# Attention and a gated layer on one core: a first load in halves on two queues, V of unit 0 by pairs, and a new layout of both weight matrices

## The chip, the cores and the metric

The kernel runs on one core of one Trainium2 chip. The metric is the device time of one execution in microseconds. The kernel before took 415.58 us (median of 3 runs, 415.23 to 416.89).

## The reference

Eight batches, 12 heads, 448 tokens, 64 numbers per head. q and k are scaled to length one per token and head; the scores are divided by tau = 0.1; softmax; times v. The result of a batch, 448 tokens by 768, is the input x of a second part with weights `w_in` (768 x 2048) and `w_out` (2048 x 768):

```python
q_n = q / (np.linalg.norm(q, axis=-1, keepdims=True) + 1e-06)
k_n = k / (np.linalg.norm(k, axis=-1, keepdims=True) + 1e-06)
attn = softmax(np.matmul(q_n, k_n.transpose(0, 1, 3, 2)) / tau)
x = concat_heads(np.matmul(attn, v))        # (3584, 768)
h = x @ w_in
g = h * np.cos(h)
return g @ w_out
```

The sum over the 2048 columns of `g` in the last product may be taken in any order, as long as the columns of `w_in` and the rows of `w_out` are grouped in the same way.

## The kernel before

**Units and pairs.** A unit is half a batch, six heads; there are 16. A pair is two heads; there are 48, six to a batch, numbered through: pairs 0 to 2 are unit 0, pairs 3 to 5 unit 1. Tokens are laid over 64 partitions in 7 blocks of 64 numbers, k on partitions 0 to 63 and q on 64 to 127 of the same tile `raw`, so one row of a token group is 1792 bytes per head.

**The stages of a pair.** `load` brings k and q into `raw` (f32). `square` squares them (on ACT for pairs 0 to 2, on POOL for most others; pair 0 in two pieces, blocks 0-3 and 4-6). `reduce` sums the squares on DVE (`n`), `rnorm` makes the inverse root by Ln and Exp on ACT (`rn`), `scale` multiplies on POOL and gives bf16 `qks`; for pair 0 the first piece is scaled on POOL and the second on DVE. `transposes` turns `qks` on TensorE (for the early pairs; copied out by DVE to `qkT`) or by DMA. `scores` (L735, L727) makes the scores in PSUM `SC`, four steps per pair, and ACT's Exp (L742) writes `PX`. `attend` multiplies with V (`va`), sums the softmax's denominators and ends in `xT`, the transposed x of a batch.

**The second part.** M1 (`m1_step`, L953) is x times W1: 16 column groups n of 128 columns, each 6 matmuls over the 768 rows, 96 a batch. W1's columns are the stationary operand. ACT takes the sine with a shift of pi/2 (`cosb`, L982), DVE multiplies it with M1's result (`gT`, L984). M2 (`m2_quarters` L1052, `m2_fill` L1081) is `gT` times W2, where one step y uses 128 rows of W2. The M2 work of a batch is spread in small runs between the score and AV matmuls of the next batch, so that TensorE has work while ACT makes exponentials. The first M2 output tile goes through y = 0 to 7 of both halves, then y = 8 to 15 of both halves.

**Loads.** k and q loads go out on the SP queue in the order of the pairs. `load_v`, `load_w1` and `load_w2` go out on POOL's queue, since they turn f32 into bf16 on the way. V is loaded a unit at a time with two DMAs. W1 comes in four loads of 512 columns, W2 in four loads of 512 rows; in each, partition p takes row 128 f + p of W2 for four values f, so a load has 512 rows of 3072 bytes. V of unit 0 waits for the first q load (key "first"); W1.0, W1.1 and V of unit 1 wait for the first piece of pair 0's scaled tile. The other weight loads are held behind `scale1.0` and `scale1.1`, the products of pairs 3 and 4.

**Order.** `Program` collects all operations with what they read and write. `arrange` plays them against a table of costs (three passes), picks for each engine the ready operation with the earliest due time, and the resulting order per engine is emitted with semaphores. A DMA has a planned volume (`bulk`) and a planned delay after it (`pad`); both move the due time of the load and the planned start of what reads it. TensorE's order is only changed within a short window. Before the first real work TensorE multiplies zeros (L1111, "filler") in its planned gaps.

Of the kernel before, what the change touches and what calls it, by code (L numbers as in the profile page):

```python
# [7 lines left out]
ALU = mybir.AluOpType  # L8
# [24 lines left out]
    "afterstep": 0,  # L33
    "single": 8,
# [43 lines left out]
class Op:  # L78
    __slots__ = ("eng", "fn", "idx", "deps", "cost", "mode", "dma", "bulk", "lock", "label", "bias",
                 "start", "end", "late", "weight", "pad", "descs", "lead", "free", "waits", "inc", "count", "pos", "dcount", "known", "nd")  # L80


class Program:
# [27 lines left out]
    def op(self, eng, fn, reads=(), writes=(), cost=0.0, mode=None, dma=None, bulk=0.0, lock=False, label="", bias=0.0):  # L111
        o = Op()
        o.eng, o.fn, o.dma, o.cost, o.mode, o.bulk, o.lock = eng, fn, dma, cost, mode, bulk, lock
        o.weight, o.pad, o.descs, o.lead = 1.0, 0.0, 0, 0.0
# [64 lines left out]
    def play(self):  # L179
# [8 lines left out]
        free["PE"] = free["SP"] = 0.7  # L188
# [54 lines left out]
        while todo:  # L243
            best = None
            for e in self.ENGINES:
                if e == "PE":
                    s = None
                    for o in pe[: self.WINDOW if pe and pe[0].free else self.REACH]:
                        if o.free != pe[0].free:
                            break  # L250
                        if left[o.idx] == 0:
                            t = max(free[e], ready_at[o.idx])
                            if not o.free and mode is not None and o.mode != mode:
                                t += self.SWITCH[o.mode]
                            if s is None or t < s - self.PATIENCE:
                                s, c = t, (t, 0, o)
# [159 lines left out]
def bass_cosine_attention__then__act_gcu_kernel(  # L416
# [85 lines left out]
    W2v = W2.ap().rearrange("p (f n) -> p f n", f=NF)  # L502
    xTv = [t.ap().rearrange("p (c m) -> p c m", c=NKC) for t in xT]
# [92 lines left out]
    def load(u, p0, p1, apart=False, eng="SP", behind=None, reads=()):  # L596
# [4 lines left out]
            for x, t in enumerate((k, q))]  # L601
        for x in ((0,), (1,)) if apart else ((0, 1),):
# [6 lines left out]
    def load_v(u, behind=None, reads=()):  # L609
# [3 lines left out]
        b, hb = u // 2, UH * (u % 2)  # L613
        dma("POOL", [lambda e, z=z: e.dma_start(  # L614
# [14 lines left out]
    def square(u, p, parts):  # L629
        i = u % 2  # L630
        for eng, t in halves(parts):
# [3 lines left out]
            src_, dst = [("raw", i, p, z) for z in range(2)], [("sq", p, z) for z in t]  # L635
            n = (w.stop - w.start) * 2 * D
            if eng == "A":
                act(lambda e, x=x, y=y: e.activation(y, x, ACT.Square), src_, dst, n, label="sq%d.%d" % (u, p))  # L638
            else:
# [33 lines left out]
    def scale(u, p, parts):  # L673
        i = u % 2
        h = slice(2 * p, 2 * p + 2)
        for eng, t in halves(parts):
# [4 lines left out]
            src_ = [("raw", i, p, z) for z in range(2)] + [("rn", i, p, z) for z in t]  # L681
            keys = [("qks", i, p, z) for z in t]
# [64 lines left out]
    def split(g, stages):  # L747
# [20 lines left out]
        for n in stages:  # L768
            P.op("PE", lambda e, c=n: part(e, c), [("va", y), ("PX", j, n + 1)], ["AVa", "AVs"], cost=MM, mode="Q", label="AV%d" % g)
            if n == 2:  # L770
                P.op("PE", tail, [("va", y), ("PX", j, 0)], ["AVa", "AVs"], cost=HALF, mode="Q", label="R%d" % g)
# [29 lines left out]
    def attend(g, direct, stages=(0, 1, 2)):  # L801
# [60 lines left out]
        for n in stages:  # L862
            if n < 2:
                o = P.op("PE", lambda e, n=n: rest(e, n), [("va", y), ("PX", j, 0), "ones", "zeros"], ["AVa", "AVs"],
# [4 lines left out]
            elif n == 3:  # L869
                for c in range(NT3):  # L870
                    P.op("PE", lambda e, c=c: quarter(e, c, 0), [("va", y), ("PX", j, c + 1), "ones"], ["AVa", "AVs"],
# [3 lines left out]
        if g in PLAN["quarters"]:  # L875
            for c in range(NT3):
                P.op("PE", lambda e, c=c: quarter(e, c, 1), [("va", y), ("PX", j, c + 1), "ones"], ["AVa", "AVs"],
                     cost=MM, mode="Q", label="AV%d" % g)
        for c in range(NT3) if g not in PLAN["quarters"] else ():
            P.op("PE", lambda e, c=c: av(e, c), [("va", y), ("PX", j, c + 1)], ["AVa"], cost=MM + (0.021 if c == 0 else 0),  # L880
# [67 lines left out]
    def m1_step(b, bank, n, c0, c1, order):  # L948
        a, (name, ph) = n % 2, PHs[bank]

        def f(e):
            for c in range(c0, c1):
                t = e.matmul(ph[:, a, 0:S], W1v[:, order[c], 128 * n : 128 * n + 128], xTv[b % 2][:, order[c], :],  # L953
# [3 lines left out]
        return P.op("PE", f, [("W1", n // 4)] + [("xT", b % 2, order[c]) for c in range(c0, c1)], BANKS.get(name, [name]),  # L957
# [140 lines left out]
    def load_w1(x, behind=None, reads=()):  # L1098
        w = FF // NQ
        dma("POOL", [lambda e: e.dma_start(  # L1100
            W1v[:, :, w * x : w * x + w], bass.AP(moe_w_in.tensor, w * x, [[FF, 128], [128 * FF, NKC], [1, w]]))],
            list(reads), [("W1", x)], "W1_%d" % x, 3.5, "W1.%d" % x, behind, 2.0)

    def load_w2(x, behind=None):
        w = NF // NQ
        dma("POOL", [lambda e: e.dma_start(
            W2v[:, w * x : w * x + w, :], moe_w_out[128 * w * x : 128 * w * (x + 1), :].rearrange("(f p) n -> p f n", p=128))],
            (), [("W2", x)], "W2_%d" % x, 3.5, "W2.%d" % x, behind, 3.0)
# [255 lines left out]
```

## Time and profile before

| | us |
|---|---|
| median of the runs | 415.58 |
| profiled execution | 415.4 |
| its span, first to last instruction | 413.6 |
| granted TensorE clock, mean | 1.000 |
| PE busy | 404.6 (98%) |
| PEld busy | 243.8 (59%) |
| ACT busy | 270.2 (65%) |
| POOL busy | 248.5 (60%) |
| DVE busy | 199.9 (48%) |

Busy PE is a modelled share: a matmul of 448 columns is shown with 352 ns, while twelve of them in a row take 2.27 us. A line such as `raw<-in_k_dram` names the tile that is written and what is read. PEld is the weight load of TensorE. The time to landing of a DMA counts from the start of its issue. GB/s counts a load that converts to bf16 with its written bytes.

Times of the start that the change touches (us from the span's start): first k load issued 0.72, first q load 1.54; ACT's table load 0.72 to 2.00; first square 5.44; V of unit 0 issued 5.65 to 7.18; first product on POOL 7.52; V of unit 1 issued at 8.86 and the first W1 load at 10.17; first score matmul 11.64; first dense M1 run 34.1; first M2 matmul 56.84. The W1 loads are issued at 10.17, 20.89, 25.08 and 30.89 and land 20.9, 15.2, 14.8 and 12.8 us later; the W2 loads at 31.77, 33.83, 36.23 and 42.00, landing 16.0, 19.4, 20.7 and 20.5 us later.

### The profile page before, as it was taken

To read this page: it belongs to the slowest core of one execution; us is meant where nothing else is said; L and a number is where in the kernel's file an instruction comes from. 1 tells how busy PE (TensorE), PEld (TensorE's weight loads), DVE (VectorE), ACT (ScalarE), POOL (GpSimd) and SP (SyncE) were. 2 spreads that over 40 slices of the span, in tenths; PEclk is the share of its full clock that TensorE was granted. 3 is DMA by queue.
4 is the path that set the end of the run, shared out by engine and by line. 5 is a ranking of instruction groups with operands and counts; after the bars stand their busy time and mean duration, and the time that the engine had idled before them with its cause. 6 is when DMAs were issued, how large, how long until landed. Compare 5 with 4: busy or idle time off the path is not lost.

```text
span 413.6 us, 13910 instructions
## 1 busy us (share of the span) xinstructions
PE 404.6 (98%) x6213; PEld 243.8 (59%) x6213; DVE 199.9 (48%) x279; ACT 270.2 (65%) x384; POOL 248.5 (60%) x196
## 2 busy tenths in 40 slices
PE   7899999999999999999999999999999999999997
PEld 3354556655566655765567656865567655655555
DVE  4574653426664457445644567344742344413421
ACT  5897578985889745985497647884488745623500
POOL 4999995894776985988489656946482303020000
PEclk9999999999999999999999999999999999999999
DMA  8999999489997999586988975797933531151023
GB/s 183 248 252 226 207 222 202 136 157 215 178 163 164 228 258 188 121 205 149 206 101 188 268 132 113 135 215 188 169 51 79 147 85 32 46 139 38 2 73 81
DMA packets 78736, 63.99 MB, mean 155 GB/s; under 512 B 41844, under 2 KB 72404, under 8 KB 78676
## 3 DMA queue, kind: packets, MB, share of 16 engines
q1 hardware_dynamic: 60468, 50.42, 54.4%
q0 software_dynamic: 18048, 12.59, 20.7%
q8 instruction: 49, 0.80, 0.8%
q10 hardware_dynamic: 160, 0.10, 0.1%
q14 instruction: 11, 0.09, 0.1%
HBM read 55.44 MB, written 11.19 MB: 161 GB/s over the span
## 4 chain that ended last, share of the span: by engine, by line
PE 91%; POOL 3%; ACT 2%; DVE 2%; DMA 1%; issue 0%; SPq 0%; ACTq 0%; POOLq 0%
PE MP L1052 27%; PE SC L953 20%; PE AV L953 12%; PE SC L727 7%; PE AV L764 5%; PE MP L1081 4%; PE AV L788 4%; PE SC L1081 3%; PE MP L953 2%; PE AV L837 2%; POOL qks L678 1%; PE SC L735 1%; ACT cosb L982 1%; PE MP L852 1%; PE AV L1081 1%; DMA raw<-in_q_dram 1%
## 5 line engine op out<-in xcount | busy, mean ns | idle before, releaser
L742 ACT ACTIVATE PX<-SC 128x448 bf16<-128x448 f32 (+1 forms) x192 | 148.7, 825 | 16.0 <-PE SC L727 10.9
L1052 PE MATMUL MP<-W,gT 64*64 64x384 bf16 x2816 | 136.2, 323 | 0.7 <-DVE qkT L716 0.6
L1052 PEld LDWEIGHTS MP<-W,gT 64*64 64x64 bf16 x2816 | 80.1, 107 | 34.5 <-issue 3.9
L953 PE MATMUL SC<-xT,W 128*128 128x448 bf16 x444 | 90.9, 353 | 0.0
L678 POOL TENSOR_TENSOR qks<-raw,rn 128x896 bf16<-128x896 f32 (+1 forms) x48 | 79.8, 1679 | 12.0 <-ACT rn L670 11.6
L640 POOL TENSOR_TENSOR sq<-raw 128x896 bf16<-128x896 f32 x44 | 73.9, 1686 | 11.8 <-DMA raw<-in_q_dram 6.4
L940 POOL TENSOR_TENSOR xT<-xu,RB 128x448 bf16<-128x448 f32 x36 | 40.1, 1135 | 67.7 <-DMA RB<-scr 67.7
L953 PEld LDWEIGHTS SC<-xT,W 128*128 128x128 bf16 x444 | 43.1, 98 | 40.2 <-ACT osb L1016 0.4
L982 ACT ACTIVATE cosb<-SC,cst 128x896 f32<-128x896 f32 x37 | 37.2, 1006 | 37.8 <-PE SC L953 35.9
L953 PE MATMUL AV<-xT,W 128*128 128x448 bf16 x276 | 59.6, 352 | 0.0
L647 DVE TENSOR_REDUCE n<-sq 128x14 f32<-128x896 bf16 (+2 forms) x49 | 51.6, 1059 | 7.1 <-ACT sq L638 4.8
L984 DVE TENSOR_TENSOR gT<-SC,cosb 128x896 bf16<-128x896 f32 x37 | 40.3, 1090 | 28.2 <-ACT cosb L982 28.1
L727 PE MATMUL SC<-qkT 64*64 64x448 bf16 x576 | 51.9, 354 | 0.3
L982 ACT ACTIVATE cosb<-AV,cst 128x896 f32<-128x896 f32 x23 | 23.1, 1006 | 37.1 <-PE AV L953 35.4
L774 DVE COPY xu<-AV 128x448 f32<-128x448 f32 x36 | 22.5, 624 | 50.4 <-PE AV L756 50.4
L953 PEld LDWEIGHTS AV<-xT,W 128*128 128x128 bf16 x276 | 26.6, 98 | 25.4 <-DVE xs L799 1.1
L764 PE MATMUL AV<-PX,va 64*64 64x448 bf16 x432 | 38.2, 349 | 0.0
L614 POOL DMA_DIRECT2D va<-in_v_dram x32 | 22.0, 694 | 22.9 <-DVE gT L984 18.2
L1019 DVE COPY osb<-MP 128x384 f32<-128x384 f32 x26 | 14.5, 558 | 43.9 <-PE MP L1052 32.8
L984 DVE TENSOR_TENSOR gT<-AV,cosb 128x896 bf16<-128x896 f32 x23 | 25.0, 1087 | 20.3 <-ACT cosb L982 20.3
L727 PEld LDWEIGHTS SC<-qkT 64*64 64x64 bf16 x576 | 16.7, 106 | 13.0 <-ACT PX L742 6.3
L775 DVE TENSOR_TENSOR xu<-xu,AV 128x448 f32<-128x448 f32 x36 | 22.4, 621 | 1.2
(84 smaller groups left out, 364.7 us busy)
## 6 DMA issues: line engine op xcount, KB each, us to landing
raw<-in_k_dram SPq DMA_DIRECT2D x48, 224.0 KB, 5.4
raw<-in_q_dram SPq DMA_DIRECT2D x48, 224.0 KB, 5.9
out_dram<-osb SPq DMA_DIRECT2D x54, 192.0 KB, 3.1
RB<-scr SPq DMA_DIRECT2D x22, 336.0 KB, 5.2
va<-in_v_dram POOLq DMA_DIRECT2D x32, 192.0 KB, 6.1
W<-in_moe_w_in_dram POOLq DMA_DIRECT2D x4, 768.0 KB, 15.0
W<-in_moe_w_out_dram POOLq DMA_DIRECT2D x4, 768.0 KB, 20.0
qkT<-qks SPq DMA_TRANSPOSE x39, 4.4
```

The lines of the kernel that those rows point to most:

```text
L640: pool(lambda e, x=x, y=y: e.tensor_tensor(y, x, x, ALU.mult), src_, dst, 0.1 + n * 1.78e-3, label="sq%d.%d" % (u, p)).pad = LATE if u > 1 ...
L647: dve(lambda e, w=w: e.tensor_reduce(out=n2v[i][:, 2 * p : 2 * p + 2, w], in_=sqv[p][:, :, w, :], axis=mybir.AxisListType.X, op=ALU.add), ...
L678: f = lambda e, s0=s0, s1=s1: e.tensor_tensor(qksv[i][:, p, s0:s1].rearrange("p s h d -> p h s d"), rawv[i][:, h, s0:s1, :], bass.AP(rn[i] ...
L727: m = e.matmul(SCv[z][BP * o : BP * o + BP, a, 0:S], t[r, c - 1 + (NT3 + 1) * o, 0:BP], t[r, :, BP : 2 * BP], start=True, stop=True)
L742: act(lambda e: e.activation(PHv[j] if c == 0 else PXv[j][:, c - 1], SCv[z][:, :, 0:n], ACT.Exp, scale=1.0 / TAU), ["SC%d" % z], [("PX", j ...
L764: m = e.matmul(AVv[64 * a : 64 * a + 64, o, 0:S], vav[y][r, 2 * p + a, c + 1, :], PXv[j][r, c, a, :], start=(c == 0), stop=False)
L940: f = lambda e, p=p: e.tensor_tensor(xTv[b % 2][:, UP * i + p, :].rearrange("p (s o m) -> p o s m", s=NB, o=2), xuv[:, u % 3, p, :].rearra ...
L953: t = e.matmul(ph[:, a, 0:S], W1v[:, order[c], 128 * n : 128 * n + 128], xTv[b % 2][:, order[c], :], start=(c == 0), stop=(c == NKC - 1))
L982: act(lambda e, ph=ph, cz=cz: e.activation(cosv[cz], ph[:, :, 0:S], ACT.Sin, bias=cst.ap()[:, 0:1], scale=1.0), names(gi) + ["cst0"], [("c ...
L984: dve(lambda e, ph=ph, cz=cz, gi=gi: e.tensor_tensor(gTv[:, 2 * gi : 2 * gi + 2, S * (b % 2) : S * (b % 2) + S], ph[:, :, 0:S], cosv[cz], ...
L1052: r = e.matmul(POH[b][x : x + 64, 0:HW], gTv[k, y, col + x : col + x + 64], W2v[k, y, HW * b : HW * b + HW], start=(y == 0 and h == 0), st ...
L1081: r = e.matmul(po[:, 0 : w[1] - w[0]], gTv[:, y, col : col + 128], W2v[:, y, w[0] : w[1]], start=(y == 0), stop=(y == NF - 1))
```

## The change

1. **Pair 0 by halves on two queues.** k is loaded by SP and q by ACT, each in two DMAs: blocks 0-3 (1024 bytes per row) and blocks 4-6 (768 bytes). The first square waits for the first halves only, the second for the second halves; `scale` likewise. ACT issues its two DMAs before its table load. The key "first" is now the landing of k's first half.
2. **V of unit 0 by pairs.** Two DMAs for pair 0, released by k's first half, and two for pairs 1 and 2, released by the first piece of pair 0's scaled tile. The AV matmuls of unit 0 wait for their own part.
3. **W2 in four-row packets.** Within a load, partition p takes the four rows 512 x + 4 p + j, j = 0 to 3, which are 12288 consecutive bytes: 128 rows a load in place of 512. So that step 4 x + j of M2 meets the right columns, M1's column group n takes W1's columns 512 (n // 4) + n % 4 + 4 p, a step of four elements in the stationary operand. W1's loads are as before.
4. **The planner's table.** A W2 load gets a planned volume of 3.07 for 3.5 and a planned delay of 10.5 for 3.0; ACT starts 0.7 later, as SP and PE do. Options that are not used here (`shy`, squares on DVE, other cuts of W1) come with it.

```diff
+    "gates": "xcccac",
+    "openers": ("SP", "ACT"),
+    "v0": ((0, 1), (1, 3)),
+    "together": 4,
+    "w1": (0, 1, 2, 3, 4),
...
-        free["PE"] = free["SP"] = 0.7
+        free["PE"] = free["SP"] = free["ACT"] = 0.7
...
+    TOGETHER = PLAN["together"]
+
+    def wide(c, n):
+        x = 128 * (n - n % TOGETHER) + n % TOGETHER
+        return W1v[:, c, x : x + 128 * TOGETHER - n % TOGETHER : TOGETHER]
...
+        if apart:
+            for z in range(2):
+                s0, s1 = blocks((z,))
+                for x, t in enumerate((k, q)):
+                    go = lambda e, x=x, t=t, s0=s0, s1=s1: e.dma_start(
+                        rawv[i][BP * x : BP * x + BP, h, s0:s1, :].rearrange("p h s d -> p h (s d)"),
+                        bass.AP(t.tensor, ((u // 2) * NH + UH * (u % 2) + 2 * p0) * S * D + s0 * D, [[NB * D, BP], [S * D, 2], [1, (s1 - s0) * D]]))
+                    dma(PLAN["openers"][x], [go], list(reads), [("part", x, z)] + (["first"] if x == 0 and z == 0 else []), "part%d_%d" % (x, z),
+                        0.97 * (s1 - s0) / NB, "load u%d p%d" % (u, p0),
+                        ([o for o in P.ops if o.eng == PLAN["openers"][x] and o.dma is not None] or [None])[-1], 1.8)
+            if "ACT" in PLAN["openers"]:
+                P.order_only([o for o in P.ops if o.eng == "ACT" and o.dma is not None][-1], [o for o in P.ops if o.label == "table"][0])
+            return
...
+        if u == 0:
+            for (p0, p1), reads in zip(PLAN["v0"], reads):
+                dma("POOL", [lambda e, z=z, p0=p0, p1=p1: e.dma_start(
+                    vav[i][BP * z : BP * z + BP, 2 * p0 : 2 * p1, 1 - z : NT3 + 2 - z, :].rearrange("p h x d -> p h (x d)"),
+                    bass.AP(v.tensor, 2 * p0 * S * D + NT3 * D * z, [[NB * D, BP], [S * D, 2 * (p1 - p0)], [1, (NT3 + 1) * D]]))
+                    for z in range(2)],
+                    list(reads), [("vp", p) for p in range(p0, p1)], "vp%d" % p0, 0.89 * (p1 - p0), "load v u0", None)
+            return
...
+            src_ += [("part", x, z) for x in range(2) for z in t] if (u, p) == (0, 0) else []
...
-                t = e.matmul(ph[:, a, 0:S], W1v[:, order[c], 128 * n : 128 * n + 128], xTv[b % 2][:, order[c], :],
+                t = e.matmul(ph[:, a, 0:S], wide(order[c], n), xTv[b % 2][:, order[c], :],
...
-            W2v[:, w * x : w * x + w, :], moe_w_out[128 * w * x : 128 * w * (x + 1), :].rearrange("(f p) n -> p f n", p=128))],
-            (), [("W2", x)], "W2_%d" % x, 3.5, "W2.%d" % x, behind, 3.0)
+            W2v[:, w * x : w * x + w, :].rearrange("p (a j) n -> p a (j n)", j=TOGETHER),
+            moe_w_out[128 * w * x : 128 * w * (x + 1), :].rearrange("(a p j) n -> p a (j n)", p=128, j=TOGETHER))],
+            (), [("W2", x)], "W2_%d" % x, 2.93 + 0.57 / TOGETHER, "W2.%d" % x, behind, 0.5 + 2.5 * TOGETHER)
...
-    first = ["first"]
-    load_v(0, None, first)
-    first = [("qks", 0, 0, 0)]
-    load_w1(0, None, first)
-    load_w1(1, None, first)
-    load_v(1, None, first)
+    opens = {"a": [("part", 0, 0)], "b": ["first"], "f": [("qks", 0, 0, 0), ("qks", 0, 0, 1)], "c": [("qks", 0, 0, 0)], "d": [("qks", 0, 1, 0)], "e": [("qks", 0, 2, 0)]}
+    load_v(0, None, [opens[x] for x in PLAN["gates"][4:]])
+    load_w1(0, None, opens[PLAN["gates"][1]])
+    load_w1(1, None, opens[PLAN["gates"][2]])
+    load_v(1, None, opens[PLAN["gates"][3]])
```

37 lines of the change are left out of this document (20 added, 17 removed).

## The prediction

> **What bounds the kernel now.** I read the busy shares by slice first, then the chain that ended last, then stretches of the span, and at the end single lines.
>
> The slices of the page (each digit a tenth busy, 40 slices of 10.3 us):
>
> ```profile
> PE   7899999999999999999999999999999999999997
> ACT  5897578985889745985497647884488745623500
> POOL 4999995894776985988489656946482303020000
> DMA  8999999489997999586988975797933531151023
> ```
>
> PE is full from the fourth slice to the last but one; POOL and the DMA engines are full in slices 2 to 6. PE's 7 and 8 at the start are partly not work: the matmuls of L1111 only keep the array busy on zeros. So the whole change can only act before PE fills up, and what it wins there is carried to the end if nothing later takes it back.
>
> The chain that ended last, in order of time (start, length, what):
>
> ```profile
> 1.54 3.81 DMA raw<-in_q_dram
> ...
> 5.44 0.64 ACT sq L638
> ...
> 6.10 0.70 DVE n L647
> ...
> 7.52 1.05 POOL qks L678
> ...
> 8.86 1.35 POOL va L614 x2
> 10.21 0.48 POOL W L1100
> ...
> 11.05 1.73 POOL qks L678
> 12.78 1.63 POOL sq L640
> 14.41 1.64 POOL qks L678
> 16.05 1.63 POOL sq L640
> 17.68 1.65 POOL qks L678
> ```
>
> It starts with the landing of pair 0's q at 5.35, goes through the norm chain to POOL, and stays on POOL (two DMA issues for V of unit 1, one for W1, then products) until 19.33; from there it runs through PE.
>
> Stretches (busy us of PE, PEld, DVE, ACT, POOL; clock; DMA share; GB/s):
>
> ```profile
> 4.40:11.00 6.60, 5.16 (x33) 2.59 (x31) 3.80 (x6) 4.21 (x10) 4.71 (x6) 1.00 1.12 230
> 11.00:19.30 8.30, 6.41 (x92) 2.58 (x89) 4.50 (x7) 7.18 (x14) 8.30 (x7) 1.00 1.20 250
> 19.30:34.10 14.80, 14.53 (x222) 8.13 (x223) 9.86 (x15) 14.02 (x26) 14.76 (x14) 1.00 1.18 255
> 34.10:49.80 15.70, 15.70 (x110) 7.83 (x107) 8.72 (x10) 10.05 (x14) 15.49 (x12) 1.00 1.24 208
> ```
>
> POOL has no idle time from 11.0 on, ACT is 87% and then 95% busy until the first dense matmuls of M1 at 34.1, and PE is full from there. The granted clock is 1.00 throughout.
>
> Weight loads and their matmuls, by line (ns min/median/max):
>
> ```profile
> L953 PEld LDWEIGHTS SC<-xT,W x444: 95/98/99, 37.7 to 386.9; 128*128 128x128 bf16 x148
> L953 PE MATMUL SC<-xT,W x444: 352/352/363, 37.9 to 387.1; 128*128 128x448 bf16 x148
> ...
> L852 PEld LDWEIGHTS MP<-RB,gT x16: 186/190/190, 19.7 to 31.1; 128*128 128x128 f32 x16
> ```
>
> M1 is 444+276+48 = 768 such matmuls. In the chain 12 of them take 2.27 us, 189 ns each, so a 98 ns load lies wholly under the matmul before it.
>
> **Part 1: pair 0 by halves on two queues.** Before: SP issues k at 0.72 and q at 1.54; by their times to landing (3.6 and 3.8) they land at 4.32 and 5.34, so 224 KB take 1.02 us (225 GB/s). After: SP issues k's blocks 0-3 (128 KB) and 4-6 (96 KB), ACT the same of q, both from about 0.72. If the two queues share that rate, both first halves are there at 4.32 - 1.02 + 2 x 0.58 = 4.47; if they run side by side, at 3.90. Bounds of the gain on 5.35: 0.88 and 1.45. I take 0.88, since all loads of this kind in 4.3 to 5.3 moved 229 GB/s together. [...]
>
> Costs: two more issues on SP, none in place of the old, since the two of q move to ACT; pairs 1 and 2 keep their issue times 2.20 to 4.15 and their landings, 7.25 and 9.25. ACT issues two DMAs before its table load: with SP's first row (0.76) and its usual 0.61, and the load's 1.28, it is free at 3.4, under the wait for data until 4.47 (1.1 us of cover; without it each us would fall on the first square). Smaller packets (1024 and 768 bytes for 1792): not shown; between nothing and, if packets cost as many as bytes do, a doubling of 0.58 to 1.16, which eats the gain. I take nothing, since W1's and W2's packets of different size (below) hardly differ.
>
> The chain from landing to the first product on POOL is 7.52 - 5.35 = 2.17, so it starts at 6.64 and ends at 7.7. For the second half, its square can start at once after the first (about 5.4 for 5.96), and its product on DVE, which stood behind the reduction of pair 1 (8.30 to 9.39) and started at 9.30, can come before that reduction, near 7.2. Then both transposes and copies are done near 8.7, and the first score, at 11.64 before, could start near 9: up to 2.7 us earlier. What is late next is pair 1: data at 7.25, square until 8.27, reduction until 9.39, then Ln and Exp (0.29 and 0.21), which before waited until 10.11 for ACT's next square. POOL could start its product at about 10.1 for 11.05: 0.95 earlier. With pair 0's exponentials out of the way, pair 1's first score (14.73 before, 0.54 of it waiting for ACT) follows its product's end (11.8) by 0.6 for transposes and 0.7 for the copy, at 13.2: 1.5 earlier. From there ACT is nearly full, so this is what reaches 34.1. Bounds: 0.95 (POOL sets the pace, PE waited only 0.18 us for it at 19.3) and 2.7 (all of the first score's gain). I take 1.5, that of the stage where ACT becomes the limit.
>
> **Part 2: V of unit 0 by pairs.** Two DMA issues more on POOL, 0.69 us each: 1.38. The first pair's two are released by k's first half, at about 3.9, and end by 5.5, in POOL's idle time before 6.64 (before: 5.65 to 7.18, in a gap too). The other two wait with both W1 issues and V of unit 1 for the first product. Between 7.7 and 10.1 POOL has 2.4 us for one V issue pair (1.35) and one of W1 (0.89). What else before stood there (V of unit 1, 1.35) falls into the full stretch, ahead of squares and products of pairs 2 to 5. Bounds: 0, if it goes where products run ahead of PE (pair 4's ended at 23.5 and its transposes ran at 25.7), and 1.35, before pair 3's product. I take 0: V of unit 1 is first used at 27.58, so it may go late. Nothing queues behind the new semaphore waits that did not queue before; AV of pair 0 at 17.19 is the only early user.
>
> **Part 3: W2 in four-row packets, W1 read with step four.** Same bytes, 512 descriptors a load become 128 of 12 KB read. With the DMA engines on weights alone, W1's 1 KB packets moved 206 GB/s (37.0 to 39.5) and W2's 1.5 KB packets 208 (50.0 to 52.5): packets 50% larger, 1% faster. Four times larger: from 0 to 2% of a load's 3.7 us (landings at 53.2 and 56.9), 0.3 us in all. The last load is the one with a user close behind: issued at 42.00, landing 20.5 later, at 62.5, used by the M2 steps at 63.51. Slack 1.0; with the start 1.5 earlier 0.5 would be short, but V's first bytes and pair 0's second queue start the DMA work over a us earlier, so I take 0 here, with 0.5 as the far end. For the order, the planner now believes each W2 load 7.5 us later (10.5 for 3.0) and so asks for it 7 us sooner: POOL may issue W2 before V of unit 2. That V landed at 49.7 and is used at 59.92; behind three more loads of 3.7 it would be 0.9 late, 2.4 with the shift. I take 0: at 32.5 V had already been chosen ahead of three of them.
>
> The step of four: no weight load in this trace has a step. Nearest rows: contiguous bf16 98 ns, f32 with twice the bytes 190. Between them nothing is seen (189 covers) or 1 ns x 768 = 0.8 us. I take 0. [...]
>
> **Sum.** 1.5 + 0 + 0: the profiled run took 415.4 (span 413.6 and 1.8 around it); 415.4 - 1.5 = **413.9**. Its 415.4 is 0.2 under the median of 415.58, within the runs' spread. 0.5%, about what a measurement can tell here, is 2.1 us: 413.5.
>
> **Rivals.**
> *All of the early start is kept.* If queues run side by side and pair 0's work leaves ACT no gap, 2.7 reaches 34.1: 415.4 - 2.7 = 412.7. For it: 1.12 us of ACT were idle in 11.0 to 19.3, and 2.4 in 4.4 to 11.0. Against it: POOL's full row. Chance 0.18.
> *The last W2 load is the next wall.* Its landing stays at 62.5, M2 waits, and only its slack is won: 414.4, or 415.0 if V and raw loads push in before it. For it: DMA share above 1.1 until 62. Against: the earlier first bytes. Chance 0.15.
> *The step slows the weight load*, the other side. In every M1 matmul, a load over 189 ns shows in full: at twice 98, 196 ns, 7 x 768 = 5.4 us, 413.9 + 5.4 = 419.3. It turns the gain to nothing at 191 ns and is slower by 0.5% from 194 on. Against it the cover of 91 ns. Chance 0.09.
> *POOL's order turns bad* (V of unit 1 before pair 3's product, or V of unit 2 behind W2): 415.3 to 416.3. Chance 0.05.
>
> **Numbers.** Forecast 0.53, with its own range 412.9 to 414.9. About two fifths of it is below 413.5. Faster: 0.18 + 0.21 = 0.39; within: 0.32 + 0.15 + 0.03 = 0.50; slower: 0.09 + 0.02 = 0.11. Range 412.4 (0.3 under the first rival) to 416.1 (bad order, with the median's 0.2): the weight rival and the thin ends stay out.
>
> **What would show it.** First square on ACT near 4.5 for 5.44; first score near 9 for 11.64; POOL's product of pair 1 near 10.1; first M1 run near 32.6; M2's first at 55.3; M1's matmuls still at 189 ns and 98 ns loads. Wrong if POOL still reaches 19.3, if PE idles just before M2's fifth or sixth run of 16, or if M1's pace is above 190.

## The result, and the profile after

The changed kernel took 418.08 us (median of 14 runs, 416.68 to 419.79); the kernel before took 415.83 beside it (14 runs, 415.23 to 416.89). The ratio is 1.0055 (95% interval 1.004 to 1.0069): slower by 0.55%, just over the half per cent that a measurement of this kernel can tell, against a forecast of 413.9 and a range of 412.4 to 416.1.

The profiled run took 416.68, with a span of 414.9 (413.6 before). It is the shortest of the 14, and its clock is 1.00, while 10 of the 14 have a mean granted clock of 0.995 or 0.996. So two things have to be explained: 1.3 us that the profile shows, and about 1 us that it doesn't. Two of the profiles read further down (pair 0's halves alone, and W1 behind V of unit 1) are of runs about 1% longer than the median of their kernel; from them only issues, landings, single waits, M1's first start and the place of a dip in the clock are read.

The slices of the page (40 of 10.4 us, each digit a tenth busy):

```profile
PE   8899979999999999999999999999999999999997
ACT  4996577895889745986497646875488735623500
POOL 5999993896776985998589657936482303012000
PEclk9999999999999999999999999999999999999999
DMA  7999999769996999585978975798934531151023
```

The start is fuller. What is new is a 7 in PE's sixth slice (52 to 62 us), where PE was full before.

The stretches that the prediction showed of before (busy us of PE, PEld, DVE, ACT, POOL; clock; DMA share; GB/s):

```profile
4.40:11.00 6.60, 6.24 (x36) 2.73 (x35) 3.97 (x7) 3.84 (x9) 5.04 (x7) 1.00 1.06 259
11.00:19.30 8.30, 7.02 (x101) 3.33 (x103) 5.05 (x7) 7.72 (x17) 7.94 (x5) 1.00 1.22 255
19.30:34.10 14.80, 14.66 (x217) 7.44 (x209) 9.55 (x15) 14.04 (x26) 14.79 (x14) 1.00 1.05 210
34.10:49.80 15.70, 15.70 (x111) 9.09 (x110) 9.10 (x11) 9.89 (x13) 14.61 (x12) 1.00 1.22 213
```

More is done up to 19.3, on PE, DVE and ACT. In the third stretch the DMA engines fall from 255 to 210 GB/s, a share of 1.05 for 1.18.

The chain that ended last, in order of time (start, length, what):

```profile
4.42 5.38 DMA raw<-in_q_dram
9.82 0.95 ACT sq L670
10.77 0.21 ACT rn L701
...
11.36 1.69 POOL qks L712
...
42.46 0.55 POOL W L1141
43.01 19.64 DMA W<-in_moe_w_out_dram
62.65 0.04 issue
62.69 0.84 PE MP L1087 x16
```

It no longer stays on POOL and PE: it goes through the last load of W2, issued at 43.0 and landed at 62.65. PE waits for it; the view of PE's waits (in all, times, longest) and its timeline (start, length, tile, count, idle before) say how long:

```profile
PE MP L1087 <- DMA W<-in_moe_w_out_dram: 2.2, 1, 2.2
```

```profile
55.32 1.49 PE L1087 MATMUL MP<-W,gT 64*64 64x384 bf16 x32 [0.40 <-DVE qkT L751]
...
58.98 0.82 PE L1087 MATMUL MP<-W,gT 64*64 64x384 bf16 x16
...
62.69 0.84 PE L1087 MATMUL MP<-W,gT 64*64 64x384 bf16 x16 [2.22 <-DMA W<-in_moe_w_out_dram]
```

The same runs in the kernel before:

```profile
56.84 1.50 PE L1052 MATMUL MP<-W,gT 64*64 64x384 bf16 x32 [0.64 <-DVE qkT L716]
...
61.23 0.82 PE L1052 MATMUL MP<-W,gT 64*64 64x384 bf16 x16
...
63.51 0.82 PE L1052 MATMUL MP<-W,gT 64*64 64x384 bf16 x16
```

M2 starts 1.52 earlier, as forecast. But PE comes to the first run that needs the last quarter of W2 at 62.69 - 2.22 = 60.47, 3.04 earlier: only 5.15 us after M2's start, where it took 6.67 before. The planner's new order has put attention work of about 1.5 us (the steps with the 128x32 tiles among them) behind this run. The landing is where it was, 62.65 for 62.5.

I follow the rest by the start of M1 in each of the eight batches, after minus before: -1.33, then +0.90, +0.92, +0.94, +1.24, +1.25, +1.27, +1.29. The start is won, the wait of 2.22 takes it back and more between batches 0 and 1 (-1.33 + 2.22 = +0.89), 0.4 is lost later, and the span is 1.3 longer.

M1's own pace (ns min/median/max):

```profile
L988 PEld LDWEIGHTS SC<-xT,W x444: 112/113/132, 36.4 to 388.2; 128*128 128x128 bf16 x148
L988 PE MATMUL SC<-xT,W x444: 352/352/381, 36.6 to 388.4; 128*128 128x448 bf16 x148
```

The stepped weight load takes 113 ns for 98, all of it under the matmul: 24 matmuls still take 4.54 us in the chain, 189 each.

Why is W2 not earlier? On POOL's timeline W1's first load is issued at 22.84, where it was issued at 10.17; W1 then lands at 31.9, 37.0, 41.2 and 45.0 (31.1, 36.1, 39.9 and 43.7 before), and W2 follows it in the same queue. The queue that POOL feeds moves nothing from 22 to 25, and 0.06 MB from 25 to 26; before, it moves 0.43 MB from 22 to 26. After, and then before (DMA share and GB/s stand last):

```profile
22.00:24.00 2.00, 2.00 (x36) 0.89 (x38) 0.99 (x2) 1.99 (x5) 2.00 (x3) 1.00 0.71 174
24.00:26.00 2.00, 1.99 (x38) 1.32 (x27) 1.25 (x2) 2.00 (x5) 1.99 (x2) 1.00 0.79 148
```

```profile
22.00:24.00 2.00, 1.82 (x32) 1.12 (x24) 1.62 (x2) 1.76 (x5) 2.00 (x2) 1.00 1.18 261
24.00:26.00 2.00, 2.00 (x41) 1.05 (x39) 1.16 (x2) 1.95 (x6) 1.98 (x3) 1.00 1.16 270
```

### The profile page after: what moved, and what is told of

It is laid out like the page before. It is cut to its first block, busy times and chain, and to the rows that moved or that the text cites. A ratio compares the mean times of both kernels' runs of the same rounds, so it can differ in the third digit from the quotient of the medians.

```text
span 414.9 us, 13898 instructions
## 1 busy us (share of the span) xinstructions
PE 405.6 (98%) x6206; PEld 256.6 (62%) x6206; DVE 200.5 (48%) x279; ACT 269.6 (65%) x384; POOL 248.8 (60%) x198
## 3 DMA queue, kind: packets, MB, share of 16 engines
q1 hardware_dynamic: 60468, 50.19, 55.3%
## 4 chain that ended last, share of the span: by engine, by line
PE 86%; DMA 6%; POOL 3%; ACT 2%; SPq 1%; DVE 1%; issue 0%; ACTq 0%; POOLq 0%
PE MP L1087 27%; PE SC L988 18%; PE AV L988 11%; PE SC L762 6%; DMA W<-in_moe_w_out_dram 5%; PE AV L799 5%; PE MP L1116 4%; PE AV L823 4%; PE SC L1116 3%; POOL qks L712 2%; PE AV L872 2%; DMA raw<-in_q_dram 1%; PE SC L770 1%; PE MP L988 1%; PE MP L887 1%; PE AV L1116 1%
## 5 line engine op out<-in xcount | busy, mean ns | idle before, releaser
L1087 PEld LDWEIGHTS MP<-W,gT 64*64 64x64 bf16 x2816 | 81.1, 107 | 36.2 <-issue 4.2
L988 PEld LDWEIGHTS SC<-xT,W 128*128 128x128 bf16 x444 | 50.0, 114 | 33.5 <-ACT osb L1051 0.4
L1017 ACT ACTIVATE cosb<-SC,cst 128x896 f32<-128x896 f32 x37 | 37.3, 1007 | 38.0 <-PE SC L988 36.1
L988 PEld LDWEIGHTS AV<-xT,W 128*128 128x128 bf16 x276 | 30.9, 114 | 21.1 <-DVE xs L834 0.9
L645 POOL DMA_DIRECT2D va<-in_v_dram x30 | 20.5, 691 | 18.5 <-DVE gT L1019 18.5
L762 PEld LDWEIGHTS SC<-qkT 64*64 64x64 bf16 x576 | 17.2, 106 | 13.6 <-ACT PX L777 7.0
```

Of the source, the lines that this page charges most:

```text
L762: m = e.matmul(SCv[z][BP * o : BP * o + BP, a, 0:S], t[r, c - 1 + (NT3 + 1) * o, 0:BP], t[r, :, BP : 2 * BP], start=True, stop=True)
L988: t = e.matmul(ph[:, a, 0:S], wide(order[c], n), xTv[b % 2][:, order[c], :], start=(c == 0), stop=(c == NKC - 1))
L1017: act(lambda e, ph=ph, cz=cz: e.activation(cosv[cz], ph[:, :, 0:S], ACT.Sin, bias=cst.ap()[:, 0:1], scale=1.0), names(gi) + ["cst0"], [("c ...
L1087: r = e.matmul(POH[b][x : x + 64, 0:HW], gTv[k, y, col + x : col + x + 64], W2v[k, y, HW * b : HW * b + HW], start=(y == 0 and h == 0), st ...
```

## The experiments

Theory A, after the first reading: V of unit 0 by pairs pushes W1's first load behind pair 4's product, the queue runs empty, and all that follows in it is late. Rivals: B, packets of four rows get less of the DMA engines beside other traffic; C, the step of four costs by itself. A fourth cause came up in the runs: the granted clock. Offsets are M1's starts against before, as above.

### Another order of the same loads: V of unit 1 late

```diff
-    "gates": "xcccac",
+    "gates": "xccdac",
```

V of unit 1 waits for pair 1's product, so W1's first two loads come first.

> The changed kernel, with one key altered: V of unit 1 waits for the product of pair 1, so that POOL has room to issue the first two W1 loads at about 9 us, as the kernel before did with one of them. Theory A (order of the weight queue: the extra V issue pushed the first W1 load from 10 to 23 us, POOL's DMA queue ran empty between, and the last W2 load, at 62.65, came 2.2 us after M2 needed it): the last W2 load lands by 60.5, PE waits under 0.3 us for it, the span is 412.0 to 412.9 and the time 413.8 to 414.8, and every run shows a clock of 1.000. Theory B (packets: four-row packets of W2 get less of the DMA engines): the wait stays at 1.5 us or more and the time above 416.5. Theory C (the step of four in the weight reads costs by itself): no wait, but still above 416.

Measured: 425.3 (ratio 1.0219, 1.0198 to 1.0239). W1 went out at 9.36 and 10.21, and V of unit 1 only at 20.44, behind 1.5 MB of weights; the first AV that waits for it runs at 36.64. M1 starts 7.87 later, and nothing waits for W2 any more. Every theory missed the size. What follows: the early order has no spare room; a load taken out of one wait goes into another.

### V of unit 0 in one piece, the rest of the change kept

```diff
-    "gates": "xcccac",
+    "gates": "xccca",
-    "v0": ((0, 1), (1, 3)),
+    "v0": ((0, 3),),
```

> The changed kernel with V of unit 0 in two DMAs again, both released by k's first half; two semaphores in place of one for a later small store, which costs nothing. Theory A: the first two W1 loads go out before pair 1's product, the last W2 load lands by 60.5, no wait above 0.3 us, 413.8 to 414.8. Theory B: a wait of 1.5 us or more, above 416.5. Theory C: no wait and above 416.

Measured: 418.42 (1.0066, 1.0049 to 1.0084). W1's first two loads go out at 9.16 and 10.02, the last of W2 lands at 60.2, and PE doesn't wait for it. So the place of W1 does follow from V by pairs. But M1 starts 0.32 later than before, not 1.3 earlier: halves on two queues win nothing at M1 without V by pairs. And the time that theory A set (413.8 to 414.8) is missed by over 3 us: without the wait for W2 this kernel is still not faster than the changed one. Behind M1's start it loses 2.8 us more, in part in PE waits of 1.1 at 235 us, with no releaser in the profile, and of 0.6 for a transpose.

### The old weight layout, the rest of the change kept

```diff
-    "together": 4,
+    "together": 1,
```

> The changed kernel with the old layout of W2 and W1 (packets of one row, no step in the weight reads, the planner's old delay); the halves and V by pairs stay, and POOL still issues the first W1 load after pair 4's product. Theory A: the wait for the last W2 load stays, 1.5 to 3 us, and the time is 417 to 419. Theory B: the wait is gone and the time is 414 to 415. Theory C: the weight loads of M1 go back from 113 to 98 ns and the time falls by over 1 us with the wait still there.

Measured: 420.16 (1.0097, 1.0079 to 1.0115), slower than the changed kernel. W1 again goes out late (24.26) and the last W2 load lands at 64.8, 2.2 later than with four rows. But theory A's wait of 1.5 to 3 us for it isn't there: the first run that needs it comes 9.1 us after M2's start, and not 5.15. M2's start and that run:

```profile
57.31 1.49 PE L1087 MATMUL MP<-W,gT 64*64 64x384 bf16 x32 [0.40 <-DVE qkT L751]
...
66.43 0.82 PE L1087 MATMUL MP<-W,gT 64*64 64x384 bf16 x16
```

This kernel differs from the changed one in the layout and its planned costs alone, so it is these that put the user near M2's start. All profiles agree: 5.0 to 5.2 us from M2's start to this run (waits left out) in the twelve with four rows, 6.7 to 9.1 in the five with single rows. What this kernel loses between batches 0 and 1 (2.4) is elsewhere, 1.93 of it in a wait for a transpose.

Its profile also shows what the kept one of the changed kernel did not:

```profile
14.00:18.00 4.00, 3.88 (x55) 1.53 (x47) 2.01 (x3) 2.87 (x5) 4.00 (x4) 0.57 1.27 237
```

The clock was 0.57 in these 4 us, after two PE waits, of 1.62 us for POOL's product and 1.52 for ACT, between 6.4 and 13.2. M1 starts 0.71 later for 1.33 earlier.

### The layout alone

Pair 0 comes whole on SP again, and V of unit 0 in one piece behind q. (In this kernel and in the one with V of unit 0 in one piece, the small scr stores count on one semaphore for each buffer and not on a shared one.)

```diff
-    "gates": "xcccac",
-    "v0": ((0, 1), (1, 3)),
+    "gates": "xcccb",
+    "v0": ((0, 3),),
...
-        free["PE"] = free["SP"] = free["ACT"] = 0.7
+        free["PE"] = free["SP"] = 0.7
...
-        if apart:
+        if False:
...
-        load(g // UP, g % UP, g % UP + 1, g < PLAN["apart"], "SP", [o for o in P.ops if o.eng == "SP"][-1] if g else None)
+        load(g // UP, g % UP, g % UP + 1, g < PLAN["apart"], "SP", P.ops[-1] if g else None)
```

> The kernel before with the new layout of W2 and W1 alone (four-row packets, step of four, the planner's new delay; first pair and V of unit 0 loaded as before). POOL issues its first W1 load at about 10 us, as before. Theory A: no wait of M2 above 0.3 us, M1 at 189 ns per matmul under 113 ns loads, time 415.2 to 416.2, the same as before. Theory B: the last W2 load lands after 63.5 and M2 waits a us or more, 416.8 or above. Theory C: no wait, and 416.8 or above.

Measured: 416.86 (1.0024, 1.0012 to 1.0035). M1 starts within 0.13 of before, the last W2 load is issued at 41.88 as before (42.00) and lands at 60.3 for 62.5. What is lost comes after 110 us, in the planner's other order on SP's queue, where a DMA transpose stands behind four broadcasts:

```profile
PE SC L770 <- DMA qkT<-qks: 2.0, 1, 2.0
```

Rival B falls, and with the pace of M1 so does C. What four rows bring can be read in all the profiles: from the landing of W1's last load to that of W2's last, with V of unit 2 between, it takes 18.3 to 18.8 us in four of the five kernels with single rows, and 16.6 to 17.6 in twelve profiles with four. The fifth has 17.2; it is the one below without fill, whose M1, with all the traffic that hangs on it, starts 2.6 later. The nearest pair is this kernel and the one before, with W1 landed at 43.4 and 43.7: 16.9 us for 18.8.

### W1's first load ahead of V, and more fill

The fill matmuls on zeros (31 in the changed kernel, 38 before) keep the array busy while PE would wait. The first of these three kernels forces W1's first load ahead of pair 1's product, the second sets the fill closer from 8 us on, the third does both.

```diff
+    P.order_only([o for o in P.ops if o.label == "W1.0"][0], [o for o in P.ops if o.label == "scale0.1"][0])
```

```diff
-            fn, y, took, room = self.filler
+            fn, y, full, room = self.filler
...
                 t, a = a + room / 2, a + room
+                took = full * (0.6 if a > 8.0 else 1.0)
```

> The changed kernel with one order forced: POOL issues W1's first load before pair 1's product, in the stretch of 10.4 to 11.4 us where it waited, and not behind pair 4's product at 22.8; V of unit 1 stays where it was. If the late first load is the cause of the 2.2 us wait for the last W2 load, that load lands at 60.5 or earlier (62.65 in the changed kernel), the wait at M2's fifth run is under 0.3 us, M1 still starts about 1.3 us before the kernel before, and a run at clock 1.00 has a span of 412.7 to 413.2 (about 414.5 to 415.0 in all). If the wait has another cause (the packets' size, the share of the DMA engines), W2's last load still lands after 62 and the time stays at 416.7 to 418. If the early dip of the clock is a second cause by itself, runs with a granted clock of 0.995 remain and are 1.5 to 2 us longer than those with 1.00.

> The changed kernel, with the fill matmuls on zeros (which keep the array busy while PE would wait) set closer from 8 us on: more of them in PE's early waits, nothing else. If the dip of the granted clock between 14 and 18 us comes from PE's early idle stretches, all runs have a clock of 0.999 to 1.000 and their median falls from 418.1 to about 416.7 (the changed kernel's runs at 1.00); the 2.2 us wait for the last W2 load stays. If the dip does not hang on PE's idle time, runs at 0.995 to 0.996 stay as many as before (11 of 14) and the median stays at 418.

> Both edits: W1's first load ahead of pair 1's product, and more fill matmuls from 8 us on. If the two causes are separate and together make up the loss, no wait for W2 over 0.3 us, every run at a clock of 0.999 or more, and a median of 414.3 to 415.0, 0.2 to 0.4% under the kernel before (415.6 to 415.8). If the fill matmuls delay real work, or if the planner's new order costs later as it did in the layout alone (2.0 us at 110 to 145), 416 to 417.

Measured: W1 ahead 424.0 (1.0189, 1.017 to 1.0209), both 423.68 (1.0195, 1.0182 to 1.0208). The planner set W1's issue at 8.08, ahead of V of pairs 1 and 2 and of V of unit 1, and PE waits for V of pairs 1 and 2, which landed at 25.60. PE's longest wait and two stretches of the kernel with W1 ahead:

```profile
PE AV L856 <- DMA va<-in_v_dram: 2.7, 1, 2.7
```

```profile
24.00:28.00 4.00, 2.28 (x32) 1.06 (x32) 0.18 (x1) 0.39 (x2) 1.03 (x1) 0.57 1.23 248
28.00:32.00 4.00, 4.00 (x40) 1.96 (x36) 1.06 (x2) 2.39 (x5) 3.09 (x2) 0.57 1.18 254
```

One wait of 2.69 us, ended at 25.65, is followed by 8 us at a mean clock of 0.57; M1 starts 7.1 later. (In the kernel with both the wait is 5.0.) So these two kernels didn't test what I meant them to test.

More fill alone: 417.2 (1.003, 1.0018 to 1.0042), and a clock of 0.999 or 1.000 in each of its 5 runs, where 10 of 14 had 0.995 or 0.996. The order on POOL is that of the changed kernel; the wait for W2 is still there, at 1.41. If that is all that the fill changed, the clock's share of the loss is 1.0055 - 1.003 = 0.25%, 1.0 us; the shorter wait (1.41 for 1.55 to 2.22) is in it too. The changed kernel's own 14 runs say the same size: the four at 0.999 or 1.000 have a median of 417.1, the ten others 418.2, though the two groups overlap.

### Pair 0's halves alone, and V by pairs alone

Each is the kernel before with one part of the change.

```diff
-    "gates": "xcccac",
+    "gates": "xcccb",
     "openers": ("SP", "ACT"),
-    "v0": ((0, 1), (1, 3)),
-    "together": 4,
+    "v0": ((0, 3),),
+    "together": 1,
```

```diff
-    "gates": "xcccac",
+    "gates": "xcccbc",
...
-    "together": 4,
+    "together": 1,
...
-        if apart:
+        if False:
```

(The second also takes back ACT's planned start and the order of the k and q loads, as the layout alone does.)

> The kernel before with pair 0 loaded by halves on two queues, and nothing else of the change: V of unit 0 in one piece, old weight layout. The prediction's part 1: M1 starts up to 1.5 us earlier than before, 414 in all. If the start is lost again without V by pairs (as in the run with V of unit 0 in one piece, where M1 started 0.3 later than before), M1 starts within 0.5 us of before and the time is 415 to 416.5. W1's first load is then issued near 10 and the last W2 load lands at 62 to 63, as before.

> The kernel before with V of unit 0 loaded by pairs and nothing else of the change (pair 0 as before, old weight layout, W1's first load issued behind pair 0's product as the planner places it). The prediction's part 2 costs it at nothing: 415.6, with M1's start within 0.3 us of before. If two more issues on POOL push W1's first load behind pair 4's product here too, the last W2 load lands 1 to 3 us later than its 62.5 and the time is 416.5 to 418.5; if they go into POOL's idle time, it lands as before.

Measured: halves alone 418.07 (1.0047, 1.0029 to 1.0065), M1 0.5 later than before; V by pairs alone 419.18 (1.007, 1.0044 to 1.0096), M1 0.18 later. In the second, W1's first load goes out at 23.78, and the last W2 load lands at 64.3: theory A's first half again, without any of the other parts. PE waits for W2 in neither: with single rows its user comes at 64.45 and 65.71, behind the landings at 62.2 and 64.3. The early start of the whole change, 0.6 to 1.3 us over three profiles, belongs to both parts together; alone, neither wins anything at M1.

### W1's first load in its old place, without and with more fill

```diff
+    P.order_only([o for o in P.ops if o.label == "load v u1"][-1], [o for o in P.ops if o.label == "W1.0"][0])
+    P.order_only([o for o in P.ops if o.label == "W1.0"][0], [o for o in P.ops if o.label == "scale0.1"][0])
```

> The changed kernel with W1's first load issued on POOL right behind V of unit 1 and ahead of pair 1's product, that is in POOL's wait from 10.4 to 11.4 us: the place that it has in the kernel before, and nothing is moved behind it but W1. V of unit 1 then lands as in the changed kernel (19 to 22 us) and PE has no wait for it. If the late first load of W1 is the cause of the 2.2 us wait, the last W2 load lands by 60.5 and the wait is under 0.3 us; the span of a run at clock 1.00 is 412.5 to 413.3 (414.3 to 415.1 in all). If W2's last load still lands after 61.5, the order of the weight queue isn't the cause. In runs with the clock dip 1.5 to 2 us more.

> The same with more fill matmuls on zeros from 8 us on, which took the clock dip out of the changed kernel. If the two causes (the weight queue's order and the clock) together make up the loss: clock 0.999 or more in every run and a median of 414.3 to 415.2, under the kernel before (415.6). If something else is given back later, 415.5 to 416.5.

Measured, without fill: 418.94 (1.0051, 1.0027 to 1.0076), single runs from 415.33 to 422.32. W1 goes out at 10.57, V of unit 1 makes PE wait 0.2, the last W2 load lands at 61.9 and the wait for it is 0.25. With fill: 415.63 beside 416.29 of the kernel before (0.9985, 0.997 to 1.0001; 12 runs, all at a clock of 0.999 or 1.000), no wait for W2 (landing 60.8, first use near 61.8). That is the kernel before again, not better than it. POOL's timeline of this kernel shows what came with it (start, length; idle before):

```profile
9.48 1.35 POOL L646 DMA_DIRECT2D va<-in_v_dram  x2
10.76 0.91 POOL L1136 DMA_DIRECT2D W<-in_moe_w_in_dram  x1
11.63 1.77 POOL L713 TENSOR_TENSOR qks<-raw,rn 128x896 bf16<-128x896 f32 x1
...
18.88 1.69 POOL L713 TENSOR_TENSOR qks<-raw,rn 128x896 bf16<-128x896 f32 x1 [0.58 <-ACT rn L705]
```

W1's issue delays pair 1's product to 11.63 (10.68 with the fill alone), pair 3's comes at 18.88 for 17.25, and M1 starts 0.15 earlier than before instead of 1.28. That the gain at the start and W1's early issue are paid from the same POOL time is argued from these rows, not shown: in the changed kernel pair 1's product ran nearly as late, at 11.36, and M1 was 1.33 early.

### Is it the empty queue? W1's first load behind pair 3's product

Here PE's order is that of the kernel with more fill; on POOL W1's issues move, and some squares with them.

```diff
+    P.order_only([o for o in P.ops if o.label == "scale1.0"][0], [o for o in P.ops if o.label == "W1.0"][0])
+    P.order_only([o for o in P.ops if o.label == "W1.0"][0], [o for o in P.ops if o.label == "scale1.1"][0])
```

> The changed kernel with the closer fill matmuls, and W1's first load issued on POOL behind pair 3's product (near 18.9 us) and not behind pair 4's (22.3). PE's order is that of the run with more fill matmuls alone. W1's first load then waits in its queue when V of unit 1 ends near 22, so the queue never runs empty, and no POOL work ahead of pair 3 moves. If an empty queue between V of unit 1 and W1 is what makes the last W2 load late, it lands 1.0 to 2.5 us earlier than 62.65, the wait at M2's fifth run falls from 2.2 (1.4 with the fill) to under 0.6, M1 still starts 1.0 to 1.3 before the kernel before, and the time is 0.3 to 0.6% under the run with more fill alone, 414.5 to 415.5. If the DMA engines are simply full (share over 1.1) and the last landing hangs on all bytes before it, the landing moves by under 0.5 us and the time stays at 416.5 to 417.3.

Measured: 417.08 (1.0036, 1.0021 to 1.005), the same as the fill alone (1.003). W1 went out at 19.48, and the queue that POOL feeds moved 0.46 MB from 22 to 26 us, where it moved 0.17 with the fill alone and 0.06 in the changed kernel. Yet the last W2 load landed at 61.7, for 61.9 with the fill alone. The wait fell to 0.86, mostly because PE reached M2 0.36 later. So theory A's second half falls: the empty queue is real, but filling it moves the last landing by 0.2.

### Does idle PE time alone lower the clock?

The kernel before without its fill matmuls from 8 us on (the same edit as above in it, with 100.0 in place of 0.6):

> The kernel before without its fill matmuls from 8 us on (some 14 of 38), and nothing else. If PE's early idle time by itself lowers the granted clock, runs show 0.995 or 0.996 for 1.000 and the time is 1 to 3 us above the kernel before (416.5 to 419). If the fill matmuls do not matter, clock 1.000 and a time within 0.5 us of before.

Measured: 419.33 (1.0076, 1.0056 to 1.0096), mean clocks of 0.988 in five runs and 0.992 in one. Its stretches of 2 us:

```profile
8.00:10.00 2.00, 0.60 (x7) 0.41 (x7) 1.82 (x3) 0.55 (x3) 1.70 (x3) 1.00 1.11 222
10.00:12.00 2.00, 0.13 (x3) 0.00 (x0) 1.04 (x2) 1.36 (x3) 1.42 (x3) 0.72 1.26 237
12.00:14.00 2.00, 1.45 (x15) 0.85 (x15) 0.38 (x2) 1.64 (x4) 2.00 (x2) 0.50 1.19 238
...
18.00:20.00 2.00, 1.93 (x25) 0.73 (x27) 1.48 (x2) 1.97 (x4) 1.86 (x3) 0.50 1.21 264
20.00:22.00 2.00, 2.00 (x36) 0.96 (x28) 0.76 (x2) 0.56 (x2) 2.00 (x3) 0.72 1.20 234
```

PE is busy 0.73 of 4 us, the mean clock is 0.72, then 0.50 from 12 to 20 us and 0.72 again, and M1 starts 2.57 later. Shown, then: with fewer fill matmuls, so with more idle PE time early on, and nothing else changed, the clock fell to 0.988 or 0.992, where all 16 runs of the kernel before beside it had 0.999 or 1.000. So the early idle time lowered the clock by itself here, and the fill matmuls are what the kernel before pays to keep it.

### Where the clock falls in the changed kernel

> The changed kernel itself, for one more profile, since the one kept has a granted clock of 1.00 and 10 of its 14 runs had 0.995 or 0.996. If the dip comes from PE's idle time at the start, the clock falls to about 0.5 to 0.6 for some 3.4 us between 12 and 20 us, and M1 starts 1.5 to 2 us later than in the kept profile. If it comes from the 2.2 us wait for the last W2 load, the low slice lies at 60 to 68 us and M1 starts at 32.7 as before.

> The same once more, with the same two expectations, in case one of the two profiles has no dip.

Measured: 417.22 and 417.63, both at a clock of 1.00, so no dip was caught. (The expected 3.4 us is an estimate from the row with single rows: 0.57 over 4 us is 0.43 x 4 / 0.5 = 3.4 us at a clock of 0.50, the lowest mean in the rows above.) They do show the wait for W2 again, 1.78 and 1.55 us (landings 62.9 and 62.4), and M1's first start 0.61 and 0.92 earlier than before. Where the dip lies in the changed kernel itself stays open. Three things speak for the start: the profile with single rows, which has the same start, has it at 14 to 18; fill matmuls, which stand only ahead of M1, went with a clock of 0.999 or 1.000 in all 28 runs of three kernels; and PE's 2.2 us wait at 60 left the clock at 1.00 in the kept profile. Against it stand two other profiles without more fill that show a dip (a mean clock of 0.996), of pair 0's halves alone and of W1 behind V of unit 1: their dip lies at 74 to 80 us, each behind a PE wait of 2.1 or 2.2 us. The second of them shares the changed kernel's start. Its stretches:

```profile
76.00:78.00 2.00, 2.00 (x32) 1.21 (x28) 0.00 (x0) 0.92 (x1) 2.00 (x3) 0.50 0.40 86
78.00:80.00 2.00, 2.00 (x40) 1.30 (x36) 0.05 (x1) 0.92 (x2) 1.63 (x1) 0.66 1.12 69
```

## Why the prediction was wrong

**What held.** The sum's first term, in the kept profile: M1 at 32.73 (32.6 forecast), M2 at 55.32 (55.3), 1.5 us won. In the two others M1 is 0.61 and 0.92 earlier and M2 0.80 and 1.11, so the term came out whole in one of three. The step of four: no run before the change had a stepped weight load; here it took 113 ns for 98, hidden by the matmul's 189, worth nothing; the rival that hung on it falls. V of unit 2 behind W2 cost nothing.

**Part 1, right in its sum, not in its steps.** The first square started at 4.08 in the kept profile, and at 4.32 and 4.42 in the two others: between the bounds of 4.47 (one shared rate) and 3.90 (side by side; the figures that I gave for it make 3.88), and not always near the one that I took. With one queue in the rows of before, the choice between the two was my estimate, and three starts from 4.08 to 4.42 don't settle it. But "pairs 1 and 2 keep their issue times" failed: SP's two half loads took 0.77 and 0.83, the next issue came at 2.42 for 2.20, and pair 2's q landed at 9.80 for 9.25. ACT, in order, had pair 2's square ahead of pair 1's Ln and waited 1.69 us for that q, so POOL's product of pair 1 started at 11.36, not at 10.1: later than before (11.05). M1 was early all the same, so that product wasn't what set it.

**Part 2 is the step that failed first.** I costed it at nothing, since "what else before stood there (V of unit 1, 1.35) falls into the full stretch". I had asked which of the displaced loads had an early user. V of unit 1 stayed (9.09). Displaced was W1's first load, whose user is not late but whose successors in the queue are: 12.7 us later out, and W1's last landing 1.3 us later.

**Part 3: two terms of opposite sign, both mis-sized.** Four-row packets were put at 0.3 us; they bring 1.2 here (17.6 for 18.8 from W1's last landing to W2's). That nearly cancels the late W1, so the last landing stayed at 62.65. Against it I set a slack of 1.0, and 0 to 0.5 of wait. The wait was 2.22 (1.55 to 2.22 over three profiles), just before M2's fifth run, where the prediction had looked for a sign of being wrong. This term is the one that lost the forecast gain. Slack and shift would have given 62.65 - (63.51 - 1.52) = 0.66; the other 1.5 is PE's order, in which the planner moved the user of W2's last quarter towards M2's start. I had read the user's time off the old order and shifted it, though the change also altered the planner's costs for W2; the kernel with single rows shows that this moved the user. So the rival "the last W2 load is the next wall" had the mechanism right, at a chance of 0.15, and its price (414.4 to 415.0) too low for the same reason.

**The clock was no part of the sum.** I noted that it was 1.00 throughout, and took that for a property of the kernel. In the kernel before it went with the fill (0.988 in five runs and 0.992 in one with less of it); 10 of 14 runs of the changed kernel (31 fill matmuls for 38, PE waits at 11 to 12 us) had 0.995 or 0.996, about 1.0 us in the median. Whether they lost it at the start isn't shown.

**What remains open.** More fill takes 0.25% and the clock's dips away together (1.0055 to 1.003), and W1's old place with the fill brings the time back to before (0.9985). That the wait for W2 eats the early start is read from M1's offsets in the changed kernel; no kernel here has the early start without the wait, and those without the wait (V of unit 0 in one piece, single rows, V by pairs alone) are no faster. Why W2's last load lands at 60.2 to 60.8 with W1 in its old place and at 61.7 with W1 behind pair 3's product, though the queue that POOL feeds moved 0.46 MB from 22 to 26 us in the latter (0.43 in the kernel before), isn't shown; one profile with W1 in its old place has 61.9. The 0.4 us lost after batch 1 isn't accounted for either.

The spread of single runs at a clock of 1.00 (415.3 to 420.1 in the kernel with W1 behind V) has one visible source: PE waiting for nothing that the profile names, 1.8 us in two places of the kernel with W1 behind pair 3, and none in the kernel before. The largest stands in PE's waits of the kernel with W1 behind V, without fill; the second line is of the DMA queues from 72.7 to 74.2 us, just ahead of it (kind of queue, packets, MB, share of the engines):

```profile
PE MP L1087 <- issue: 2.2, 1, 2.2
q8 instruction: 1, 0.02, 5.5%
```

The traces do say what goes with such waits. All 20 of them above 0.2 us, in 12 of the 17 profiles, end 1.2 to 1.6 us after a 16 KB packet on this queue of instructions. That PE was then waiting for its own instructions is my estimate from these 20 cases; no run here was built to test it.

## What to carry to other kernels

Where a planner or scheduler makes the order, a user's time can't be read off the old order and shifted: a change to the cost of one load moves both its landing and its user, and the slack between them is worth nothing as an estimate. When two issues are added ahead of a queue, ask not which displaced load has the nearest user, but which has the longest tail of loads behind it (here W1's first, 12.7 us later out). And a clock of 1.00 in one profile is not a fact for all runs: the changed kernel had 1.00 in the kept profile and 0.995 or 0.996 in 10 of 14 runs, and in the profile with single rows, which has the same quick start, the clock was 0.57 from 14 to 18 us and M1 started 0.71 later, not 1.33 earlier.

## What the runs showed of the hardware that was not expected

**The granted clock fell in pieces of about one length.** The lowest mean clock of a stretch was 0.50, in the kernel before with less fill and with W1 behind V. If that is the low clock of each fall, the lost clock divided by one half is an estimate of the time at it: 0.43 x 4 us / 0.5 = 3.4 us with single rows, (0.50 + 0.34) x 2 / 0.5 = 3.4 at 76 to 80 us with W1 behind V, 0.43 x 8 / 0.5 = 6.9 after the 2.69 us wait, and in the kernel before with less fill (0.28 x 4 + 0.5 x 8) / 0.5 = 10.2. These are one, two and three times 3.4, in four profiles. Ahead of the falls stood PE waits of 2.69 us in one piece, or of 1.62 and 1.52 with 3.7 us between them. One of 2.22 us stood ahead of the fall near 75 us with W1 behind V, and one of 2.22 at 60 us in the changed kernel had no fall behind it; so no length of wait that decides it was shown.

**Stepped weight reads took 15 ns more.** 113 ns for 98 at a step of 8 bytes between bf16 values, over all 768 loads of M1; with 189 ns of matmul above each it doesn't show.

**Larger packets shortened the loads more than the old rows let expect.** In the kernel before, packets of 1 KB and 1.5 KB (as written) moved 206 and 208 GB/s. Four rows make 6 KB, and from 55.0 to 56.5 us, where both kernels load W2 alone, they moved 221 GB/s (62 packets, 0.33 MB) for 209 (211 packets, 0.31 MB). Four loads of 768 KB then take 14.2 us for 15.1, an estimate from these rates. Among other traffic the stretch of W2's loads went from 18.3 to 18.8 us in most profiles to 16.6 to 17.6. One profile with single rows has 17.2, so not all of the difference is shown to come from the packets.
